# SwiGLU feed-forward block: the first weight loads wait for the issue of x, and the first two gate groups run ahead of the up groups

## The chip, the cores and the metric

The kernel runs on one core of a Trainium2 chip. The metric is the device time of the program in microseconds (us). A core has TensorE (PE in the profile, with its weight loads shown apart as PEld), VectorE (DVE), ScalarE (ACT), GpSimd (POOL) and SyncE (SP). In this kernel SP and ACT issue all the DMAs. Their transfers run on 16 shared DMA engines, from one queue for each issuer: q1 for SP and q10 for ACT.

## The reference

The inputs are bf16: x of [1, 2048, 512], w_gate and w_up of [512, 1376], w_down of [1376, 512].

```python
def reference(x, w_gate, w_up, w_down):
    g = _silu(x @ w_gate)
    u = x @ w_up
    return (g * u) @ w_down
```

## The kernel before, in words

**Layout.** TensorE multiplies along the partitions, so x is needed transposed: `xT_sb` holds it as four slices of 128 features (dk = 0 to 3) by 2048 tokens. The tokens are cut into four chunks of 512. `w_sb` holds w_gate and, behind it, w_up. The 1376 hidden features are ten full tiles of 128 (ft = 0 to 9) and a rest of 96, which is packed into groups of its own ("X" and "Y").

**Groups.** A group is one PSUM bank's worth of work. For a full tile and a chunk there is a gate group ("G") and an up group ("U"), each of four matmuls of 128x128 weights against 512 columns of x. ScalarE takes silu of the gate bank (L280), and VectorE multiplies this with the up bank into `hT_sb` (L289). After all chunks come the groups of the down projection ("O", L394 and L408), whose banks are copied to `o_sb` (L293) and stored by SP (L258). There are 8 banks, used in turn.

**Loads.** The first 256 tokens of x are loaded untransposed into `xn_sb` (L108), and TensorE transposes them by an identity matrix (L346). The second 256 tokens come by a transposing DMA named `x0b` (`load_x`, L87), as do the later chunks. The weights come in slabs of tiles, a gate half and an up half each: `wg0` and `wu0` are tile 0, `wg1` and `wu1` tile 1, then tiles 2 and 3, 4 to 6, and 7 to the end (`load_w`, L92). ScalarE issues `wg0` and `wu0` as the first thing it does (`loads_on_scalar`), and then loads its activation table and runs a dummy activation (L269). SyncE issues everything else in this order (`loads_on_sync`): `xn`, `wg1`, `wu1`, `x0b`, the other slabs, the x of the later chunks, and w_down. An engine issues in the order of its program; a `wait_ge` ahead of an issue holds whatever stands behind it on that engine.

**TensorE's opening** (`on_tensor`). First come N_WARM = 6 matmuls of 512 columns and N_FILL = 2 of 128 on constants (L337), whose results are not used. Then TensorE waits for the identity and for `xn`, and does eight 128x128 transposes (L346): for the token pieces i = 0 and 1 (128 tokens each) and the halves h = 0 and 1 of the features. Each pair goes to a bank, and VectorE (h = 0) or ScalarE (h = 1) copies it to `xT_sb`. The four first groups, g0, u0, g1 and u1 (gate and up of tiles 0 and 1, chunk 0), then run by pieces of columns through `gu_matmuls(g, n0, n1)` (L328): g0 on piece 0 and on piece 1 (4 matmuls of 128 columns each), u0 likewise, then g1 and u1 on both pieces at once (4 matmuls of 256 columns each), and last the second half (tokens 256 to 511, from `x0b`) of g0, u0, g1 and u1, 4 matmuls of 256 columns each. From there the groups run whole. `need(name)` makes TensorE wait for a load when it is first used, and `after` for a copy; both are waits of the first matmul that needs them. No planner decides this order: it is as written.

Of the kernel before, what the change touches and what calls it, by code (L numbers as in the profile page):

```python
# [6 lines left out]
BF16 = mybir.dt.bfloat16  # L7
FP32 = mybir.dt.float32

N_WARM = 6  # L10
N_FILL = 2


def bass_standalone__swiglu_ffn__prompt_kernel(nc, x, w_gate, w_up, w_down, out):
    _, S, D = x.shape
    F = w_gate.shape[1]
    P = 128
# [11 lines left out]
    HT = SC // 2  # L29
    NXN = HT // P  # L30
# [14 lines left out]
    with ExitStack() as es:  # L45
        sb = lambda name, shape, dt: es.enter_context(nc.sbuf_tensor(name, shape, dt))
        ps = lambda name, shape, dt: es.enter_context(nc.psum_tensor(name, shape, dt))
        sem = lambda name: es.enter_context(nc.semaphore(name))
# [18 lines left out]
        diag = sb("diag", [P, P], mybir.dt.int32)  # L67

        s_I = sem("s_I")
        s_J = sem("s_J")  # L70
        s_P = sem("s_P")
        s_A = sem("s_A")
# [4 lines left out]
        def load_sem(name):  # L77
            loads[name] = sem(f"s_{name}")
            return loads[name]
# [6 lines left out]
        def load_x(eng, name, t0, t1):  # L86
            eng.dma_start_transpose(  # L87
                xT_sb[:, :, t0:t1], xf[t0:t1, :]
            ).then_inc(load_sem(name), 16)

        def load_w(eng, name, src, base, f0, f1):
            eng.dma_start(  # L92
                w_sb[:, :, base + f0:base + f1],
                src[:, f0:f1].rearrange("(k p) f -> p k f", p=P),
            ).then_inc(load_sem(name), 16)
# [4 lines left out]
        def load_slab(eng, a, b):  # L100
            load_w(eng, f"wg{a}", w_gate, 0, a * P, min(b * P, F))
            load_w(eng, f"wu{a}", w_up, UPH, a * P, min(b * P, F - 32))

        def loads_on_scalar(act):
            load_slab(act, *slabs[0])

        def loads_on_sync(sp):
            sp.dma_start(  # L108
                xn_sb[:, :, :].rearrange("p j d -> p (j d)"), xf[0:HT, :].rearrange("(p j) d -> p (j d)", j=NXN)
            ).then_inc(load_sem("xn"), 16)  # L110
            load_slab(sp, *slabs[1])
            load_x(sp, "x0b", HT, SC)
            for a, b in slabs[2:]:
                load_slab(sp, a, b)
            load_w(sp, "wut", w_up, F - (F - 32), F - 32, F)
            for c in range(1, NSC):
                load_x(sp, f"x{c}", c * SC, (c + 1) * SC)
            sp.dma_start(
                wd_sb[:, 0:NFF, :], w_down[0:NFF * P, :].rearrange("(k p) d -> p k d", p=P)
            ).then_inc(load_sem("wd"), 16)  # L120
            for c in range(NSC):
                sp.dma_start(
                    wdt_sb[R * c:R * (c + 1), :, :], w_down[NFF * P:F, :].rearrange("(q p) d -> p q d", p=R)
                ).then_inc(load_sem(f"wdt{c}"), 16)
            sp.dma_start(wdl_sb[:, :], w_down[NFF * P:F, LASTA:D]).then_inc(load_sem("wdl"), 16)
# [7 lines left out]
        def add_group(kind, **what):  # L133
            g = dict(kind=kind, at=len(groups), bank=banks[len(groups) % NB], readers=[], **what)
            groups.append(g)
            return g
# [71 lines left out]
        for i in range(NXN):  # L208
            for h, eng in enumerate("DA"):
                g = add_group("T", i=i, h=h)  # L210
                op = add_op(
                    eng, g, kind="copy", out=xT_sb[:, 2 * h:2 * h + 2, i * P:(i + 1) * P],
# [15 lines left out]
        for at in range(NST):  # L228
# [5 lines left out]
            for c0, c1 in halves:  # L234
                g = add_group("O", t=t, c0=c0, c1=c1, c=c)
                if c0 == 0:
                    quads[j].append(g)
                else:
# [3 lines left out]
                    eng, g, kind="copy", out=o_sb[ob][:, c0:c1], src=g["bank"][:, 0:c1 - c0],  # L242
# [11 lines left out]
        def on_sync(sp):  # L254
            loads_on_sync(sp)
            for t, c0, c1, ob, eng, n in stores:
                sp.wait_ge(s_A if eng == "A" else s_D, n)
                sp.dma_start(rows_of(t)[:, c0:c1], o_sb[ob][:, c0:c1]).then_inc(s_out[ob], 16)  # L258
            for i in range(NOS):
                sp.wait_ge(s_out[i], 16 * n_store[i])  # L260
# [6 lines left out]
        def on_scalar(act):  # L267
            loads_on_scalar(act)
            act.activation(adummy[:, 0:4], zero_c, ACT.Silu)  # L269
            for op in act_ops:  # L270
                act.wait_ge(s_P, op["g"]["at"] + 1)
                if op["kind"] == "silu":
                    if op["free"]:
                        act.wait_ge(s_D, op["free"])
                    fn = ACT.Silu
                else:
                    if op["stored"][1]:
                        act.wait_ge(*op["stored"])
                    fn = ACT.Copy
                act.activation(op["out"], op["src"], fn).then_inc(s_A, 1)  # L280
# [15 lines left out]
        def on_tensor(pe):  # L296
            landed = set()

            def need(name):
                if name not in landed:  # L300
                    pe.wait_ge(loads[name], 16)
                    landed.add(name)
# [3 lines left out]
            def after(eng, n):  # L306
                if n > read[eng]:
                    pe.wait_ge(s_A if eng == "A" else s_D, n)
                    read[eng] = n
# [6 lines left out]
            def gu_matmuls(g, n0, n1):  # L316
                c, ft = g["c"], g["ft"]
                if c > 0:
                    need(f"x{c}")
                if c == 0 and n1 > HT:  # L320
                    need("x0b")
                need(("wg" if g["kind"] == "G" else "wu") + str(slab_of[ft]))
                col = (0 if g["kind"] == "G" else UPH) + ft * P
                for dk in range(KD):
                    if c == 0 and dk % 2 == 0:
                        for i in range(n0 // P, min(n1 // P, NXN)):
                            after(*xt_ready[i, dk // 2])
                    ins = pe.matmul(  # L328
                        g["bank"][:, n0:n1], lhsT=w_sb[:, dk, col:col + P],
                        rhs=xT_sb[:, dk, c * SC + n0:c * SC + n1], start=(dk == 0), stop=(dk == KD - 1),  # L330
                    )
                if n1 == SC:
                    ins.then_inc(s_P, 1)

            def warm(n, width):
                for i in range(n):
                    pe.matmul(banks[NB - 1][:, 0:width], lhsT=ones_w, rhs=ones_m[:, 0:width], start=True, stop=True)  # L337

            warm(N_WARM, SC)
            warm(N_FILL, P)  # L340
# [6 lines left out]
                ins.then_inc(s_P, 1)  # L347

            g0, u0, g1, u1 = groups[NT:NT + 4]
            for g in (g0, u0):  # L350
                gu_matmuls(g, 0, P)
                gu_matmuls(g, P, HT)
            gu_matmuls(g1, 0, HT)
            gu_matmuls(u1, 0, HT)
            for g in (g0, u0, g1, u1):
                gu_matmuls(g, HT, SC)
# [80 lines left out]
        on_gpsimd(nc.gpsimd)  # L437
        on_scalar(nc.scalar)
        on_tensor(nc.tensor)
        on_vector(nc.vector)  # L440

# [27 lines left out]
```

## Time and profile before

| what | value |
|---|---|
| median of 3 runs | 120.57 us (120.52 to 120.98) |
| the profiled execution's own time | 120.32 us |
| its span, first to last instruction | 118.9 us (so 1.42 us lie around it) |
| TensorE matmul busy | 115.4 us (97%) |
| TensorE weight loads busy | 54.1 us (45%) |
| VectorE, ScalarE busy | 47.3 us (40%), 31.0 us (26%) |
| SP queue q1, ACT queue q10 | 8.48 MB, 0.26 MB |

How to read the views used below. All times count from the span's start. A row of the timeline is the start, the duration, the engine with the source line, the operation with output<-inputs and shape, the number of instructions merged into the row, and in brackets the idle time before it and what ended that. An engine name with a q (SPq, ACTq) is its issue of a DMA, not the transfer. A row of the stretch view is a stretch A:B with its length, then each engine's busy time and instructions, then the granted clock, the DMA engines' mean busy share, and the GB/s moved. The DMA view gives packets and MB by queue. Matmul ends are modelled, and matmuls overlap, so the starts of weight loads (PEld) are the better clock of TensorE.

### The profile page before, as it was taken

What the parts mean: (1) busy time and instruction counts of PE and PEld (TensorE: products, weight loads), DVE (VectorE), ACT (ScalarE), POOL (GpSimd) and SP (SyncE); (2) the same over time, 40 slices, a digit from 0 to 9 for tenths busy, and PEclk for the clock granted to TensorE, in tenths of its full rate; (3) what the DMA queues carried; (4) which work ended last, traced back from release to release, by engine and by line L of the source; (5) the groups of instructions that cost most, each with busy time, mean ns of one, the idle gap of its engine ahead of it and who ended that gap; (6) DMA issues with size and microseconds to landing.
All of it is one profiled execution on the core that took longest, in us unless ns stands there. A gap on an engine that the chain in (4) does not pass through costs nothing.

```text
span 118.9 us, 1519 instructions
## 1 busy us (share of the span) xinstructions
PE 115.4 (97%) x600; PEld 54.1 (45%) x611; DVE 47.3 (40%) x73; ACT 31.0 (26%) x53; POOL 0.4 (0%) x5
## 2 busy tenths in 40 slices
PE   7999999999999999999999999999999999999993
PEld 2774444444444444444444444344434444444452
DVE  0133443353443444433444334469617422006530
ACT  4344324454234363244262343230000000000001
POOL 1000000000000000000000000000000000000000
PEclk9999999999999999999999999999999999999999
DMA  3999999970000000000000000000004221002412
GB/s 103 271 307 357 264 162 242 328 183 24 0 0 0 6 0 0 0 3 3 0 0 0 6 0 0 0 0 0 0 0 138 88 88 44 0 0 75 145 50 88
DMA packets 17559, 8.84 MB, mean 74 GB/s; under 512 B 10640, under 2 KB 17424, under 8 KB 17552
## 3 DMA queue, kind: packets, MB, share of 16 engines
q1 hardware_dynamic: 16496, 8.48, 26.7%
q10 hardware_dynamic: 1056, 0.26, 1.0%
q8 instruction: 5, 0.08, 0.3%
q14 instruction: 2, 0.02, 0.1%
HBM read 4.81 MB, written 2.10 MB: 58 GB/s over the span
## 4 chain that ended last, share of the span: by engine, by line
PE 97%; issue 1%; DVE 0%
PE bank L328 58%; PE bank L394 29%; PE bank L370 3%; PE bank L337 2%; PE bank L408 2%; PE bank L381 2%; PE bank L346 1%; DVE o_sb L293 0%; PE bank L431 0%
## 5 line engine op out<-in xcount | busy, mean ns | idle before, releaser
L328 PE MATMUL bank<-xT_sb,w_sb 128*128 128x512 bf16 (+2 forms) x338 | 69.7, 364 | 0.4
L328 PEld LDWEIGHTS bank<-xT_sb,w_sb 128*128 128x128 bf16 x344 | 32.8, 98 | 36.4 <-issue 0.2
L289 DVE TENSOR_TENSOR hT_sb<-sg_sb,bank 128x512 bf16<-128x512 f32 x40 | 27.5, 688 | 40.5 <-PE bank L328 36.6
L394 PE MATMUL bank<-wd_sb,hT_sb 128*128 128x512 bf16 (+2 forms) x166 | 34.5, 366 | 0.4 <-issue 0.3
L280 ACT ACTIVATE sg_sb<-bank 128x512 f32<-128x512 f32 x40 | 23.8, 596 | 40.8 <-PE bank L328 40.8
L394 PEld LDWEIGHTS bank<-wd_sb,hT_sb 128*128 128x128 bf16 x170 | 16.1, 98 | 19.1 <-issue 1.3
L293 DVE CAST o_sb<-bank 128x512 bf16<-128x512 f32 (+1 forms) x16 | 10.1, 663 | 22.0 <-PE bank L408 12.3
L280 ACT ACTIVATE o_sb<-bank 128x384 bf16<-128x384 f32 x1 | 0.5, 492 | 37.8 <-PE bank L394 37.8
L289 DVE TENSOR_TENSOR ht_sb<-sgy_sb,bank 32x512 bf16<-32x512 f32 x8 | 5.5, 684 | 0.2
L289 DVE TENSOR_TENSOR ht_sb<-sgx_sb,bank 32x512 bf16<-32x512 f32 x4 | 2.8, 691 | 3.5 <-ACT sgx_sb L280 3.5
L370 PE MATMUL bank<-xT_sb,w_sb 128*128 128x512 bf16 x15 | 4.1, 379 | 0.1
L337 PE MATMUL bank<-const-bfloat16-1.0 128*128 128x512 bf16 (+1 forms) x8 | 2.9, 545 | 0.8 <-PEq L454 0.8
L280 ACT ACTIVATE sgx_sb<-bank 32x512 f32<-32x512 f32 x4 | 2.4, 588 | 4.5 <-PE bank L370 4.5
L408 PE MATMUL bank<-wdt_sb,ht_sb 32*128 32x512 bf16 (+1 forms) x48 | 2.9, 372 | 0.0
L370 PEld LDWEIGHTS bank<-xT_sb,w_sb 128*128 128x128 bf16 x16 | 1.6, 98 | 1.9
L280 ACT ACTIVATE sgy_sb<-bank 64x512 f32<-64x512 f32 x4 | 2.4, 590 | 0.1
L337 PEld LDWEIGHTS bank<-const-bfloat16-1.0 128*128 128x128 bf16 x8 | 1.0, 136 | 2.4 <-issue 2.4
L381 PE MATMUL bank<-xT_sb,w_sb 128*64 128x512 bf16 x16 | 1.9, 382 | 0.0
L408 PEld LDWEIGHTS bank<-wdt_sb,ht_sb 32*128 32x128 bf16 x48 | 1.1, 93 | 1.7 <-issue 0.8
L269 ACT ACT_TABLE_LOAD x1 | 1.3, 1283 | 1.8 <-issue 1.8
L293 DVE COPY xT_sb<-bank 128x256 bf16<-128x256 bf16 x2 | 0.6, 292 | 2.7 <-PE bank L346 2.7
L381 PEld LDWEIGHTS bank<-xT_sb,w_sb 128*64 128x64 bf16 x16 | 0.8, 109 | 1.0 <-DVE hT_sb L289 0.4
(14 smaller groups left out, 4.0 us busy)
## 6 DMA issues: line engine op xcount, KB each, us to landing
out_dram<-o_sb SPq DMA_DIRECT2D x15, 128.0 KB, 1.7
wd_sb<-in_w_down_dram SPq DMA_DIRECT2D x1, 1280.0 KB, 9.2
w_sb<-in_w_gate_dram SPq DMA_DIRECT2D x1, 480.0 KB, 5.9
w_sb<-in_w_up_dram SPq DMA_DIRECT2D x1, 448.0 KB, 6.5
w_sb<-in_w_gate_dram SPq DMA_DIRECT2D x1, 384.0 KB, 4.5
w_sb<-in_w_up_dram SPq DMA_DIRECT2D x1, 384.0 KB, 5.1
wdt_sb<-in_w_down_dram SPq DMA_DIRECT2D x4, 96.0 KB, 7.5
xn_sb<-in_x_dram SPq DMA_DIRECT2D x1, 256.0 KB, 2.8
```

What stands on the lines that cost most here:

```text
L269: act.activation(adummy[:, 0:4], zero_c, ACT.Silu)
L280: act.activation(op["out"], op["src"], fn).then_inc(s_A, 1)
L289: ins = dve.tensor_tensor(op["out"], op["a"], op["b"], ALU.mult)
L293: ins = dve.tensor_copy(op["out"], op["src"])
L328: ins = pe.matmul(g["bank"][:, n0:n1], lhsT=w_sb[:, dk, col:col + P], rhs=xT_sb[:, dk, c * SC + n0:c * SC + n1], start=(dk == 0), stop=(dk ...
L337: pe.matmul(banks[NB - 1][:, 0:width], lhsT=ones_w, rhs=ones_m[:, 0:width], start=True, stop=True)
L346: ins = pe.transpose(tview(g["bank"])[:, k, :], xn_sb[:, g["i"], dk * P:(dk + 1) * P], ident[:, :])
L370: ins = pe.matmul(g["bank"][:, :], lhsT=w_sb[:, dk, XC0:XC0 + P], rhs=xT_sb[:, dk, c * SC:(c + 1) * SC], start=(dk == 0), stop=(dk == KD - 1),
L381: ins = pe.matmul(g["bank"][y0:y1, :], lhsT=w_sb[:, dk, YC0:YC0 + 64], rhs=xT_sb[:, dk, c * SC:(c + 1) * SC], start=(dk == 0), stop=(dk == ...
L394: ins = pe.matmul(g["bank"][:, 0:c1 - c0], lhsT=hT_sb[:, fk, t * P:(t + 1) * P], rhs=wd_sb[:, fk, c0:c1], start=(start and fk == 0), stop= ...
L408: ins = pe.matmul(g["bank"][:, 0:c1 - c0], lhsT=ht_sb[R * c:R * (c + 1), q, j * P:(j + 1) * P], rhs=wdt_sb[R * c:R * (c + 1), q, c0:c1], s ...
```

## The change

One warm-up matmul of 512 columns is removed. ScalarE waits for a new semaphore `s_K` ahead of its first weight load; SyncE counts it up right behind its issue of `xn`, ahead of `wg1`. And the first halves run in another order: g0 and g1 on piece 0, g0 and g1 on piece 1 (16 matmuls of 128 columns), then u0 and u1 on both pieces at once (8 matmuls of 256 columns). The numbers of matmuls of each width stay as they were, apart from the warm-up; the second halves keep their order.

```diff
-N_WARM = 6
+N_WARM = 5
...
+        s_K = sem("s_K")
...
         def loads_on_scalar(act):
+            act.wait_ge(s_K, 1)
             load_slab(act, *slabs[0])
...
             ).then_inc(load_sem("xn"), 16)
+            sp.sem_inc(s_K, 1)
             load_slab(sp, *slabs[1])
             load_x(sp, "x0b", HT, SC)
...
             g0, u0, g1, u1 = groups[NT:NT + 4]
-            for g in (g0, u0):
-                gu_matmuls(g, 0, P)
-                gu_matmuls(g, P, HT)
-            gu_matmuls(g1, 0, HT)
+            for i in range(NXN):
+                for g in (g0, g1):
+                    gu_matmuls(g, i * P, (i + 1) * P)
+            gu_matmuls(u0, 0, HT)
             gu_matmuls(u1, 0, HT)
             for g in (g0, u0, g1, u1):
                 gu_matmuls(g, HT, SC)
```

## The prediction, made before the changed kernel ran

> **What bounds the kernel now.** I read the page first: the chain of work that ended last is 97% PE and the slowest groups are PE's own. So past the opening the kernel is one stream of matmuls, and the change, which touches only the opening, can move the end only by the moment from which that stream runs without a hole. I then read the timeline of the opening:
>
> ```profile
> 0.73 0.46 ACTq L92 DMA_DIRECT2D w_sb<-in_w_gate_dram  x1
> 0.74 0.40 SPq L108 DMA_DIRECT2D xn_sb<-in_x_dram  x1
> ...
> 1.20 0.41 SPq L92 DMA_DIRECT2D w_sb<-in_w_gate_dram  x1
> 1.22 0.53 ACTq L92 DMA_DIRECT2D w_sb<-in_w_up_dram  x1
> ...
> 1.66 0.50 SPq L92 DMA_DIRECT2D w_sb<-in_w_up_dram  x1
> 1.78 1.28 ACT L269 ACT_TABLE_LOAD   x1 [1.78 <-issue]
> ...
> 2.20 1.69 SPq L87 DMA_TRANSPOSE xT_sb<-in_x_dram  x1
> ...
> 3.29 0.15 PEld L337 LDWEIGHTS bank<-const-bfloat16-1.0 128*128 128x128 bf16 x1 [0.28 <-issue]
> 3.60 0.63 PEld L346 LDWEIGHTS bank<-ident,xn_sb 128*128 128x128 bf16 x8 [0.16 <-issue]
> ...
> 4.22 0.66 ACT L280 ACTIVATE xT_sb<-bank 128x256 bf16<-128x256 bf16 x2 [0.94 <-PE bank L346]
> 4.44 1.81 PEld L328 LDWEIGHTS bank<-xT_sb,w_sb 128*128 128x128 bf16 x24 [0.21 <-issue]
> ...
> 6.42 7.47 PEld L328 LDWEIGHTS bank<-xT_sb,w_sb 128*128 128x128 bf16 x44 [0.17 <-DMA xT_sb<-in_x_dram]
> ```
>
> The reader is to see three starts: transposes at 3.60, the first gate matmul behind the load at 4.44, and the second halves at 6.42. The bracket of the last row is the point of the case: PE stood waiting for x0b. The DMA view says that x0b landed 4.2 us after its issue, 2.20 + 4.2 = 6.4. So PE had nothing to do until x0b came, if only just: the last of the 24 loads ends at 4.44 + 1.81 = 6.25, its matmul of 256 columns then runs for 0.11 (the pace is worked out below), to about 6.37, so the hole is 0.05 us. **Whatever is gained ahead of 6.37 is given back at x0b.** Later loads are early: wg2 lands near 7.2 (issue 3.94 and 3.3), and is due behind 16 matmuls of 256 columns, near 8.2.
>
> What sets x0b? Its queue is SP's: xn, wg1, wu1, x0b, 768 KB, beside 256 KB of ACT's. The stretches show how the 1 MB moves, and the queues of two windows, 0 to 2.5 us and 2.5 to 3 us, who moved it:
>
> ```profile
> 1.50:2.00 0.50, 0.50 (x2) 0.15 (x1) 0.00 (x0) 0.22 (x1) 0.00 (x0) 1.00 0.29 102
> 2.00:2.50 0.50, 0.50 (x3) 0.21 (x2) 0.00 (x0) 0.50 (x1) 0.00 (x0) 1.00 1.05 320
> 2.50:3.00 0.50, 0.50 (x3) 0.22 (x2) 0.00 (x0) 0.50 (x1) 0.00 (x0) 1.00 0.86 199
> 3.00:3.50 0.50, 0.50 (x4) 0.16 (x2) 0.00 (x0) 0.27 (x2) 0.00 (x0) 1.00 1.07 229
> 3.50:4.00 0.50, 0.50 (x6) 0.40 (x5) 0.00 (x0) 0.00 (x0) 0.00 (x0) 1.00 1.26 285
> 4.00:4.50 0.50, 0.43 (x7) 0.29 (x6) 0.46 (x2) 0.28 (x2) 0.00 (x0) 1.00 1.28 286
> ```
> ```profile
> q1 hardware_dynamic: 103, 0.21, 26.8%
> q10 hardware_dynamic: 1, 0.00, 0.0%
> ```
> ```profile
> q10 hardware_dynamic: 196, 0.05, 44.9%
> q1 hardware_dynamic: 35, 0.05, 41.1%
> ```
>
> From 3.5 us the engines move a level 286 GB/s. By 2.5 us, 103 of the 128 packets of xn (2 KB each) are through and ACT's queue has only just begun; from 2.5 to 3 xn's last 25 share the engines with 196 small packets of wg0, at 199 GB/s.
>
> **The change part by part.**
>
> *The wait.* SP's issue of xn ends at 0.74 + 0.40 = 1.14. SP's steps from one issue to the next are 0.06, so I take 0.06 for the count and 0.06 for ACT's waking: ACT issues wg0 at 1.26 instead of 0.73, 0.53 later. Bounds: 1.14 (nothing for either) and about 1.4. SP's own issues, wg1 to all later ones, move by 0.06, x0b to 2.26. Behind ACT's wait stand wg0, wu0, the table load and the dummy activation: the table's end moves from 3.06 to 3.59, the dummy's (0.20) to 3.81. ACT's first copy was at 4.22 and could come at about 3.85 now, so this still hides, by 0.04; without that cover ACT's copies would be late by what is missing.
>
> *xn.* Alone, its last 25 packets (50 KB at 320 GB/s, 0.16 us) are through at 2.66 rather than beyond 3.0. xn landed at 0.74 + 2.8 = 3.54. I take 3.15; the bounds are 3.1 and 3.54 (no gain).
>
> *The warm-up matmul.* Loads of the 512-wide warm-up are 0.43 apart (2.86, 3.29), so one less ends PE's filler at about 3.07 instead of 3.50. With xn at 3.15 the transposes start at about 3.2, 0.4 earlier, and end near 4.1 (eight at a quarter of 0.43); with the copies' 0.2 behind them gate 0 could start near 4.3. Bounds: a gain of 0.43, or nothing where xn stays at 3.54.
>
> *wg0.* It landed 3.2 after its issue: now 1.26 + 3.2 = 4.46, and with 0.09 from landing to the first matmul, as for xn (3.54 to 3.63), gate 0 starts at 4.55, where it was 4.47. So the 0.4 of the transposes is not cashed: **the wait moves the stop from x to wg0.** Bounds: 4.3 (wg0 comes no later than the copies), and 5.0 if wg0 and wg1, now issued in the same instant, split the engines (128 KB more at 286 GB/s is 0.46).
>
> *The order.* Same matmuls, so it costs nothing itself; it moves due dates. At the later full pace (229 matmuls in the 49.79 busy us of 20 to 70, 0.217 for 512 columns, so 0.054 for 128 and 0.109 for 256) the first halves take 16 x 0.054 + 8 x 0.109 = 1.74 us; before they took 6.37 - 4.47 = 1.90 with small waits for copies. wg1 is now due behind 4 matmuls, 4.77, and lands at 1.26 + 3.4 = 4.66: 0.1 of cover, where it had 0.9. wu0 is due at 4.55 + 0.87 = 5.42 and lands at 1.75 + 3.7 = 5.45: a hole of 0.03 at most by these rows. wu1 is due at 5.87 and lands at 5.42. So PE reaches the second halves at 6.29 (4.55 + 1.74) to 6.45 (+ 1.90).
>
> *x0b.* The megabyte ahead of its landing is the same, and so is the start at 1.8. ACT's first packet came at 2.50, 1.77 after its issue; the same interval now gives 3.03. wg1's packets came about 3.0 (SP's other 10 packets of that window are the most there can be before), and now come near 3.1. So between 2.66 and 3.03 the engines would stand idle, and at 3.0 they are 196 x 256 B = 50 KB behind, 0.18 us at 286 GB/s. In 3.0 to 3.5 two queues now start together and can make up at most (286 - 229) x 0.5 = 28 KB, 0.10 us. That leaves +0.08 to +0.18; I take **+0.12**. Bounds: if the 1.77 was only a place in a line, so that wg1 moves up, the engines could run level from 2.5, and (286 - 199) x 0.5 + (286 - 229) x 0.5 = 72 KB come 0.25 us earlier; at the other end the whole 0.53 and SP's 0.06 stay idle, +0.59. The value lies nearest to the packets' own rows.
>
> [...]
>
> **The sum.** PE resumes at the later of x0b (6.42 + 0.12 = 6.54) and its own arrival (6.29 to 6.45): 6.54, 0.12 later. Behind it nothing differs. The profiled execution took 120.32 (118.9 of span, 1.42 around it), so 120.44; the median of the runs lies 0.25 above it, and by the median it is 120.57 + 0.12, about **120.7 us**.
>
> **The rivals.**
> 1. *The engines fill sooner* (wg1 takes the place of wg0): x0b up to 0.25 earlier, and wg0 by 4.4. For it: xn is alone, and two queues start together. Against it: of SP's 35 packets from 2.5 to 3, 25 are xn's, so at most 10 of wg1's 512 moved before 3.0, though it was issued at 1.20. 120.3 to 120.57. Chance 0.22.
> 2. *The weights collide*: wg0 and wg1 split the engines, gate 0 starts at 5.0, arrival 6.8, or x0b takes the whole delay. For it: wg1's cover has shrunk to 0.1. Against it: wu0's later due date. +0.3 to +0.59, 120.9 to 121.2. Chance 0.13.
> 3. *The clock comes later* (the slower side). TensorE starts at half pace: 0.43 for 512 columns against 0.217 later, although the clock column reads 1.00. It doubles inside the transposes: five of their loads take 3.60 to 4.05, the last two are 0.06 apart. So 3.2 us after the first matmul at 0.77 the clock was granted. If the shorter filler no longer earns it, it comes 3.2 us later, at 7.2; from 4.55 to 7.2, 2.65 us at half pace lose 1.3 us: 120.57 + 1.3 = 121.9. It decides at about 4.0 us. [...] Against it: the busy time to 4.0 stays about the same. Chance 0.10. [...]
> 4. *It doesn't do what it says*: xn lands at 3.54 all the same. Then PE idles 0.47 ahead of the transposes, and gate 0 starts near 4.55 as by wg0. The time is the forecast's, and is counted with it.
>
> **How the numbers follow.** Forecast, +0 to +0.3: 0.55. The range runs from rival 1 less 0.1 for the runs' own spread, 120.2, to the top of rival 2, 121.2; it leaves out rival 3 and small tails. A measurement of this kernel can tell about 0.5% (0.6 us) from no change. Faster by that needs more than any bound here: 0.03. Slower: rival 3 and a tail of rival 2, 0.12. Within: 0.85.
>
> **What would show it.** Right: ACT's first issue near 1.26, transposes near 3.2, first gate matmul near 4.55 behind wg0, and PE's load at the second halves near 6.54, ended by x0b. Wrong: gate 0 near 4.3; a hole before the 5th or 17th matmul (wg1, wu0) over 0.1; 512-wide pace not reached by 4.5; or second halves that start without x0b in the bracket.

## The result, and the profile after

The changed kernel takes 121.12 us (median of 20 runs, 120.69 to 122.6), the kernel before 120.61 us (20 runs, 120.28 to 121.31). The ratio is **1.0037, 95% interval 1.0021 to 1.0053**: slower by 0.45 us, 0.25 to 0.64. The forecast was 0.12 us slower. (Runs in a slower state that executions here can fall into, one at 122.6 us here and three of 12 near 123.2 in the experiment of the wait alone, stand in the medians but not in the ratios.)

The profiled execution took 121.02 us with a span of 119.6, 0.7 more than before. (That of before, 120.32 us, lies 0.29 below its median, so the two profiles differ by more than the medians do.) The timeline of its opening, the rows that answer to those shown of before:

```profile
0.74 0.40 SPq L110 DMA_DIRECT2D xn_sb<-in_x_dram  x1
...
1.22 0.50 ACTq L93 DMA_DIRECT2D w_sb<-in_w_gate_dram  x1
1.25 0.39 SPq L93 DMA_DIRECT2D w_sb<-in_w_gate_dram  x1
...
1.74 0.55 ACTq L93 DMA_DIRECT2D w_sb<-in_w_up_dram  x1
...
2.25 1.70 SPq L88 DMA_TRANSPOSE xT_sb<-in_x_dram  x1
...
3.82 0.77 PEld L349 LDWEIGHTS bank<-ident,xn_sb 128*128 128x128 bf16 x8 [0.81 <-issue]
...
4.67 1.37 PEld L331 LDWEIGHTS bank<-xT_sb,w_sb 128*128 128x128 bf16 x16
...
6.25 7.70 PEld L331 LDWEIGHTS bank<-xT_sb,w_sb 128*128 128x128 bf16 x49 [0.21 <-DMA w_sb<-in_w_up_dram]
```

Three things are to be seen. The filler ends earlier, but the transposes start at 3.82 where they started at 3.60: x did not come sooner, and TensorE idles 0.81 us for it. The 16 loads of the gate pieces start at 4.67. And the stop that ends last is no longer x0b: the bracket at 6.25 names the up half of tile 0, **wu0**. From there the first halves of u0 and u1 still have to run, 8 x 0.109 = 0.87 us, so the second halves start at 7.12, 0.70 later than the 6.42 of before: the whole 0.7 us of the span. Only the sixteen gate matmuls could run ahead of it. x0b was late too: it landed at 2.25 + 4.8 = 7.05, so it would by itself have held the second halves to about the same moment.

The DMA view of the issues up to 3 us, with the KB and the time from issue to landing, has the reason:

```profile
xn_sb<-in_x_dram SPq DMA_DIRECT2D x1, 256.0 KB, 3.0
w_sb<-in_w_gate_dram ACTq DMA_DIRECT2D x1, 128.0 KB, 3.3
...
w_sb<-in_w_up_dram SPq DMA_DIRECT2D x1, 128.0 KB, 4.0
w_sb<-in_w_up_dram ACTq DMA_DIRECT2D x1, 128.0 KB, 4.5
xT_sb<-in_x_dram SPq DMA_TRANSPOSE x1, 4.8
```

wu0 was issued 0.52 later than before (1.74 against 1.22) and then took 4.5 instead of 3.7 us; x0b took 4.8 instead of 4.2. The stretches of after show when the engines slowed (the last two columns are their busy share and GB/s):

```profile
1.50:2.00 0.50, 0.50 (x2) 0.15 (x1) 0.00 (x0) 0.00 (x0) 0.00 (x0) 1.00 1.03 57
2.00:2.50 0.50, 0.50 (x3) 0.21 (x2) 0.00 (x0) 0.18 (x1) 0.00 (x0) 1.00 0.39 86
2.50:3.00 0.50, 0.50 (x4) 0.22 (x2) 0.00 (x0) 0.50 (x1) 0.00 (x0) 1.00 0.92 333
3.00:3.50 0.50, 0.28 (x3) 0.01 (x1) 0.00 (x0) 0.50 (x1) 0.00 (x0) 1.00 1.22 301
...
4.00:4.50 0.50, 0.50 (x7) 0.50 (x6) 0.24 (x1) 0.03 (x1) 0.00 (x0) 1.00 1.05 222
4.50:5.00 0.50, 0.50 (x8) 0.33 (x6) 0.34 (x2) 0.46 (x2) 0.00 (x0) 1.00 1.11 243
5.00:5.50 0.50, 0.50 (x7) 0.50 (x7) 0.00 (x0) 0.28 (x1) 0.00 (x0) 1.00 1.41 248
5.50:6.00 0.50, 0.50 (x11) 0.50 (x8) 0.00 (x0) 0.00 (x0) 0.00 (x0) 1.00 1.25 204
```

and those of before behind 4.5 us:

```profile
4.50:5.00 0.50, 0.50 (x8) 0.37 (x9) 0.12 (x1) 0.38 (x2) 0.00 (x0) 1.00 1.28 287
5.00:5.50 0.50, 0.50 (x11) 0.50 (x11) 0.00 (x0) 0.00 (x0) 0.00 (x0) 1.00 1.29 279
5.50:6.00 0.50, 0.50 (x8) 0.45 (x6) 0.00 (x0) 0.00 (x0) 0.00 (x0) 1.00 1.11 250
```

From 2.5 to 3.5 us, where I feared idle engines, they moved more than before (333 and 301 GB/s against 199 and 229), but from 1.5 to 2.5 less (57 and 86 against 102 and 320). The two nearly cancel: over these 2 us the mean is 194 GB/s against 212, and the kernels without the wait lie on both sides of it (188 to 217 in seven profiles). The larger loss comes from 4.0 on: 222, 243, 248 and 204 against 286, 287, 279 and 250. In the window 4.5 to 6 us before, ACT's queue had 2 packets left; here it has 469, so wu0 (ACT's queue) now overlaps the transposing x0b (SP's queue).

### The profile page after: what moved, and what is told of

Read it like the earlier page. It is cut to its first block, busy times and chain, and to the rows that moved or that the text cites. A ratio compares the mean times of both kernels' runs of the same rounds, so it can differ in the third digit from the quotient of the medians.

```text
span 119.6 us, 1529 instructions
## 1 busy us (share of the span) xinstructions
PE 116.3 (97%) x610; PEld 54.5 (46%) x610; DVE 47.2 (40%) x73; ACT 31.1 (26%) x53; POOL 0.4 (0%) x5
## 4 chain that ended last, share of the span: by engine, by line
PE 95%; DMA 2%; DVE 0%; issue 0%
PE bank L331 58%; PE bank L397 29%; PE bank L373 3%; DMA xn_sb<-in_x_dram 2%; PE bank L411 2%; PE bank L384 2%; PE bank L349 1%; DVE o_sb L296 0%; PE bank L434 0%
## 5 line engine op out<-in xcount | busy, mean ns | idle before, releaser
L331 PEld LDWEIGHTS bank<-xT_sb,w_sb 128*128 128x128 bf16 x344 | 33.3, 99 | 36.3 <-DMA w_sb<-in_w_up_dram 0.2
L397 PE MATMUL bank<-wd_sb,hT_sb 128*128 128x512 bf16 (+2 forms) x170 | 35.1, 367 | 0.0
L296 DVE CAST o_sb<-bank 128x512 bf16<-128x512 f32 (+1 forms) x16 | 10.1, 663 | 22.0 <-PE bank L411 12.3
L373 PEld LDWEIGHTS bank<-xT_sb,w_sb 128*128 128x128 bf16 x16 | 1.6, 98 | 1.9
L349 PE MATMUL bank<-ident,xn_sb 128*128 128x128 bf16 x8 | 1.0, 305 | 0.6 <-DMA xn_sb<-in_x_dram 0.6
```

Source lines behind the costliest of these rows:

```text
L296: ins = dve.tensor_copy(op["out"], op["src"])
L331: ins = pe.matmul(g["bank"][:, n0:n1], lhsT=w_sb[:, dk, col:col + P], rhs=xT_sb[:, dk, c * SC + n0:c * SC + n1], start=(dk == 0), stop=(dk ...
L349: ins = pe.transpose(tview(g["bank"])[:, k, :], xn_sb[:, g["i"], dk * P:(dk + 1) * P], ident[:, :])
L373: ins = pe.matmul(g["bank"][:, :], lhsT=w_sb[:, dk, XC0:XC0 + P], rhs=xT_sb[:, dk, c * SC:(c + 1) * SC], start=(dk == 0), stop=(dk == KD - 1),
L397: ins = pe.matmul(g["bank"][:, 0:c1 - c0], lhsT=hT_sb[:, fk, t * P:(t + 1) * P], rhs=wd_sb[:, fk, c0:c1], start=(start and fk == 0), stop= ...
```

## The experiments

Two theories stood against each other. **Theory A**: the wait makes the loss, by the lateness of wu0 and x0b. **Theory B**: the shorter filler makes the loss, because TensorE's full pace (0.217 us for 512 columns instead of 0.43) is granted later. All comparisons are with runs of before on the same chip; a ratio of 1.001 is 0.12 us. What the expectations call a look is one profiled execution.

### The wait alone, and the order alone

The wait and the count alone, in the kernel before:

```diff
         def loads_on_scalar(act):
+            act.wait_ge(s_K, 1)
             load_slab(act, *slabs[0])
...
+            sp.sem_inc(s_K, 1)
             load_slab(sp, *slabs[1])
```

> Before plus the wait alone (six warm-up matmuls, old order). Theory A (the wait moves wg0 and wu0 behind SP's loads, and PE stands for wu0 and x0b): slower than before by 0.3 to 0.6 us; more in the old order than in the new, since u0 is due 0.45 us earlier here: PE stands about 1 us ahead of u0. Theory B (one warm-up matmul less lets PE idle ahead of the transposes, and the full pace comes late): within 0.15 us of before, full pace reached by about 4.2 us.

Measured: 121.33 us, ratio **1.0054 (1.0034 to 1.0075)**, +0.65 us. Theory A is borne out in kind: the timeline has TensorE standing for wu0, at u0's first half, right behind the first eight gate matmuls. It stands 0.53 us, half of what was expected, and the loss is a little above the expected range.

```profile
4.66 0.78 PEld L331 LDWEIGHTS bank<-xT_sb,w_sb 128*128 128x128 bf16 x8
5.97 2.09 PEld L331 LDWEIGHTS bank<-xT_sb,w_sb 128*128 128x128 bf16 x24 [0.53 <-DMA w_sb<-in_w_up_dram]
```

The order alone, in the kernel before:

```diff
-            for g in (g0, u0):
-                gu_matmuls(g, 0, P)
-                gu_matmuls(g, P, HT)
-            gu_matmuls(g1, 0, HT)
+            for i in range(NXN):
+                for g in (g0, g1):
+                    gu_matmuls(g, i * P, (i + 1) * P)
+            gu_matmuls(u0, 0, HT)
```

> Before with the new order of the first halves alone. Both theories: within 0.15 us of before; wg1 (landing near 4.6) is due at about 4.7, so a stop of up to 0.1 us ahead of the fifth matmul may show, hidden by x0b near 6.4.

Measured: 120.54 us, ratio 1.0003 (0.9984 to 1.0022). As expected, the order costs nothing by itself.

### Each of the other two parts taken back

After without the wait and the count:

```diff
-            act.wait_ge(s_K, 1)
...
-            sp.sem_inc(s_K, 1)
```

> After without the wait and the count (five warm-up matmuls and the new order stay). Theory A: back to before within 0.15 us, whatever PE idles ahead of the transposes, since wg0 lands near 3.9 and x0b near 6.4 as before. Theory B: slower than before by 0.3 to 0.5 us, the pace of weight loads doubles only near 5.7 us.

Measured: 120.84 us, ratio 1.0010 (0.9984 to 1.0036), single runs from 120.19 to 121.48. wu0 and x0b landed as before, near 4.9 and 6.4. In its profile the pace of weight loads doubled only near 6.7 us, and that execution took 121.15. The median favours theory A, the profile shows the late full pace of theory B, and the interval excludes neither.

After with the sixth warm-up matmul back:

```diff
-N_WARM = 5
+N_WARM = 6
```

> After with the sixth warm-up matmul back (wait and new order stay). Theory A: as slow as after, 0.3 to 0.6 us above before, with PE standing ahead of u0 for wu0. Theory B: back to before within 0.15 us, full pace near 4.0 us.

Measured: 120.85 us, ratio **1.0020 (1.0002 to 1.0037)**, +0.24 us: half of after's loss is left, between the two theories. The profiled execution was the fastest of the 12 (120.39 us, span 119.1), and it shows hardly any loss: the first gate load waits for wg0, and the second halves for x0b, at 6.46, which is the course that the prediction drew. wu0 took 3.7 us and x0b 4.2, as before, with the same loads issued at the same moments as in after.

```profile
4.49 1.79 PEld L331 LDWEIGHTS bank<-xT_sb,w_sb 128*128 128x128 bf16 x24 [0.29 <-DMA w_sb<-in_w_gate_dram]
6.46 1.53 PEld L331 LDWEIGHTS bank<-xT_sb,w_sb 128*128 128x128 bf16 x15 [0.18 <-DMA xT_sb<-in_x_dram]
```

Yet the two transfers overlapped here too. By 4.5 us SP's queue had moved 1177 packets. The 128 of xn and the 512 each of wg1 and wu1 make 1152, so nearly all that followed is x0b. The stretch from 4.5 to 5 us, and its queues:

```profile
4.50:5.00 0.50, 0.48 (x9) 0.49 (x10) 0.10 (x1) 0.36 (x2) 0.00 (x0) 1.00 1.28 286
q1 hardware_dynamic: 290, 0.07, 64.7%
q10 hardware_dynamic: 288, 0.07, 63.1%
```

x0b and the last packets of wu0 ran side by side at 286 GB/s.

By the medians: set beside the wait in the old order (+0.65), the new order gives back 0.41 us. Where wu0 sets the end, that is what it should: behind u0's start the old order has 8 x 0.054 + 8 x 0.109 = 1.31 us of first halves left, the new one 0.87, and the difference is 0.44.

### The filler by itself

```diff
-N_WARM = 6
+N_WARM = 5
```

> Before with five warm-up matmuls alone. Theory A (the wait is all of the loss): within 0.1 us of before. Theory B (the shorter filler makes the full pace come later on average): slower by 0.1 to 0.3 us, with single runs up to 121.5, since the pace doubled only near 6.7 us in the look at the kernel without the wait.

Measured: 120.72 us, ratio 1.0017 (0.9998 to 1.0036), +0.20 us, -0.02 to +0.43: inside theory B's range, and not quite clear of nothing. So I took the dose:

```diff
-N_WARM = 6
+N_WARM = 2
```

> Before with two warm-up matmuls instead of six, nothing else: the dose of theory B. The filler ends near 1.8 us and TensorE idles till xn lands near 3.5. Theory B: the full pace is granted only about 3.2 us after the transposes start, near 6.8, and from 4.5 to 6.8 half the work is lost: slower by 0.7 to 1.3 us. Theory A: within 0.15 us of before, since xn, wg0 and x0b land as before.

Measured: 122.0 us, ratio **1.0109 (1.0071 to 1.0147)**, +1.3 us. The filler matters. The stretches of its profile, 6.5 to 8.7 and 8.9 to 10.1 us, show the step: 11 weight loads in 2.20 us, then 12 in 1.20, on matmuls of one width (256 columns), although the clock column says 1.00 in both.

```profile
6.50:8.70 2.20, 2.20 (x12) 1.53 (x11) 0.00 (x0) 0.00 (x0) 0.00 (x0) 1.00 1.03 275
8.90:10.10 1.20, 1.20 (x14) 1.07 (x12) 0.32 (x1) 0.75 (x2) 0.00 (x0) 1.00 1.06 353
```

### A second profile of each kernel

The kernel before, unchanged:

> Before, unchanged, for a second look at it. If the moment of the full pace is fixed by the program, it doubles near 4.0 us again, as in the first look. If it is luck between executions, it comes anywhere up to some 3 us later, and the execution is longer by half of what it comes after 4.5.

Measured: 120.64 us with a span of 119.2. The pace doubled near 5.5 us, not 4.0: the moment moves between executions of one kernel, and this execution took 0.3 us more. After, unchanged:

> After, unchanged, for a second look. Theory B: the pace of weight loads doubles later than in any look with six warm-up matmuls (3.9 to 5.5 us), as it did in the three with five (5.7, 6.4, 6.7). Theory A: xn near 3.6, no earlier than without the wait; wu0 between 5.4 and 6.2, after its due date, and x0b at 6.4 to 7.0.

Measured: 120.99 us, span 119.6. Here theory B's expectation **failed**: the pace doubled near 4.1 us, about as early as in the first profile of before, and the execution was as long as the first. Its timeline:

```profile
4.46 1.01 PEld L331 LDWEIGHTS bank<-xT_sb,w_sb 128*128 128x128 bf16 x16 [0.20 <-DMA w_sb<-in_w_gate_dram]
6.23 1.86 PEld L331 LDWEIGHTS bank<-xT_sb,w_sb 128*128 128x128 bf16 x18 [0.77 <-DMA w_sb<-in_w_up_dram]
```

The 16 gate loads now take 1.01 instead of 1.37 us, and TensorE then stands 0.77 instead of 0.21 us for wu0, until 6.23 instead of 6.25. In both profiles of after wu0 is the last stop, and an earlier full pace is given back at that wait. (xn landed 2.8 after its issue, at 3.5; wu0 4.4 after, x0b 4.7. x0b came at 2.25 + 4.7 = 6.95, only some 0.1 ahead of the moment to which wu0 held the second halves.)

### What makes wu0 and x0b late

The wait between ScalarE's two loads, so that wg0 goes out early and wu0 late:

```diff
-            load_slab(act, *slabs[0])
+            a, b = slabs[0]
+            load_w(act, f"wg{a}", w_gate, 0, a * P, min(b * P, F))
+            act.wait_ge(s_K, 1)
+            load_w(act, f"wu{a}", w_up, UPH, a * P, min(b * P, F - 32))
...
-            load_slab(sp, *slabs[1])
+            a, b = slabs[1]
+            load_w(sp, f"wg{a}", w_gate, 0, a * P, min(b * P, F))
+            sp.sem_inc(s_K, 1)
+            load_w(sp, f"wu{a}", w_up, UPH, a * P, min(b * P, F - 32))
```

> Before (six warm-up matmuls, old order) with the wait between ScalarE's two loads: wg0 goes out at 0.73 as before, wu0 waits for a count that SyncE makes behind the issue of wg1, so that it goes out near 1.7, where the whole wait put it. If the lateness of wu0 makes the loss of the wait (theory A in its narrow form): gate 0 starts near 4.45, PE stands 0.4 to 0.8 us ahead of u0, and the time is 0.4 to 0.7 us above before, as with the whole wait in the old order. If it is wg0's lateness or the engines' idle time at the front: within 0.2 us of before.

Measured: 120.77 us, ratio 1.0020 (1.0001 to 1.0038), +0.24 us. Less than the narrow form of theory A asked for, more than its opposite: wu0 landed at 5.5, 3.8 after its issue, and TensorE stood 0.24 us for it; x0b landed at 6.7. So a late issue of wu0 alone makes about a third of the loss of the whole wait. There wu0 took 4.2 us and came at 5.9; what slowed it this run does not tell. But it has a slow stretch of its own:

```profile
5.00:5.50 0.50, 0.44 (x6) 0.13 (x3) 0.00 (x0) 0.10 (x1) 0.00 (x0) 1.00 1.38 181
q1 hardware_dynamic: 355, 0.09, 137.6%
```

181 GB/s, with SP's queue alone: ACT's last packet had gone by 5.0. So in this profile the engines slowed beside x0b with nothing in the other queue.

wu0 moved to SyncE's queue, between wg1 and wu1, in the kernel of the wait alone:

```diff
         def loads_on_scalar(act):
             act.wait_ge(s_K, 1)
-            load_slab(act, *slabs[0])
+            a, b = slabs[0]
+            load_w(act, f"wg{a}", w_gate, 0, a * P, min(b * P, F))
...
             sp.sem_inc(s_K, 1)
-            load_slab(sp, *slabs[1])
+            a, b = slabs[1]
+            load_w(sp, f"wg{a}", w_gate, 0, a * P, min(b * P, F))
+            a, b = slabs[0]
+            load_w(sp, f"wu{a}", w_up, UPH, a * P, min(b * P, F - 32))
+            a, b = slabs[1]
+            load_w(sp, f"wu{a}", w_up, UPH, a * P, min(b * P, F - 32))
```

> The kernel of e1 (wait, six warm-up matmuls, old order), but wu0 issued by SyncE between wg1 and wu1, and so in one queue with x0b; ScalarE issues wg0 alone, behind the wait. If in the looks with the wait wu0's packets were held up beside the transposing transfer of x0b in the other queue: wu0 lands near 5.0 to 5.4, PE stands under 0.4 us ahead of u0, and the time is 0.1 to 0.4 us above before instead of e1's 0.65. If it is the late issue of wg0 and the engines' start that cost: 0.5 us or more above before, since x0b is also issued 0.5 us later.

Measured: 121.0 us, ratio 1.0031 (1.0013 to 1.0048), +0.37 us, in the range that the side-by-side reading asked for. TensorE never stood for wu0, and the engines moved 271 GB/s from 4 to 6 us, like the kernels without the wait. x0b took 3.9 us instead of 4.6 to 4.8, but it was also issued 0.54 later, at 2.79, and so landed at 6.7, near the 6.85 of the wait alone. Everything behind x0b on SyncE had moved back as well, and the loss reappears there, at tile 2's gate weights (issued at 4.58 instead of 3.94, and 4.3 instead of 3.3 us from issue to landing):

```profile
8.93 0.55 PEld L337 LDWEIGHTS bank<-xT_sb,w_sb 128*128 128x128 bf16 x4 [0.53 <-DMA w_sb<-in_w_gate_dram]
9.68 0.23 PEld L337 LDWEIGHTS bank<-xT_sb,w_sb 128*128 128x128 bf16 x2 [0.20 <-DMA w_sb<-in_w_up_dram]
```

So this run moves the loss to another place and does not decide between the two readings.

### x with the engines to itself

```diff
+            sp.wait_ge(loads["xn"], 16)
             sp.sem_inc(s_K, 1)
```

> The kernel of e1 (wait, six warm-up matmuls, old order), with SyncE also waiting until xn has landed before it counts and issues anything else, so that xn has the DMA engines to itself. If sharing with wg0 made xn late (the step of the prediction), xn lands near 3.1. If xn's time is its own, it lands near 3.5 to 3.7, as in all looks with and without the wait. The weights and x0b come some 2.5 us late, so the time is 2 to 3 us above before and says nothing.

Measured, one execution (124.29 us): **xn landed 2.8 us after its issue, at 3.5**, as without the wait. The DMA view of 0 to 3 us has SP's queue only, and xn still took as long:

```profile
q1 hardware_dynamic: 136, 0.25, 25.6%
issues: line engine op xcount, KB each, median us to landing
xn_sb<-in_x_dram SPq DMA_DIRECT2D x1, 256.0 KB, 2.8
```

So in this execution there was nothing for the wait to win. Its profile also shows the clock itself, in its column (third from the right) of three stretches:

```profile
3.65:7.05 3.40, 1.01 (x16) 0.84 (x16) 0.51 (x2) 2.04 (x4) 0.00 (x0) 1.00 0.74 157
7.07:10.46 3.39, 2.81 (x20) 2.10 (x18) 0.00 (x0) 0.00 (x0) 0.00 (x0) 0.50 1.19 274
10.48:14.00 3.52, 3.47 (x26) 2.38 (x25) 1.38 (x2) 1.79 (x3) 0.00 (x0) 1.00 1.09 371
```

It was granted near 3.6 (the loads of its eight transposes, from 3.64, take 0.46 us where the first profile of before needed 0.63), taken away after 3.4 us in which TensorE had been busy for 1.01, and granted again 3.4 us later. The dates of the full pace in two profiles of one kernel lie 1.5 us apart for before (4.0 and 5.5) and 1.6 for after (5.7 and 4.1). What sets the date within one kernel was not shown.

### An attempt to do better

```diff
-N_FILL = 2
+N_FILL = 4
...
                 ins.then_inc(s_P, 1)
+            warm(2, P)
```

> Before with two more 128-wide filler matmuls behind the warm-up and two behind the transposes, in stretches where TensorE stood idle (3.50 to 3.60 and 4.24 to 4.44 in the first look). Theory B: the full pace comes earlier on average, and the time is 0.05 to 0.3 us below before. If the filler only delays the transposes and gate 0, at half pace by up to 0.2 us each: 0.1 to 0.3 us above before. Theory A says nothing on it.

Measured: 120.66 us, ratio 1.0009 (0.9991 to 1.0027): no difference that these runs can tell. The pace doubled near 5.5 us in its profile. No version here is shown to beat the kernel before.

## Why the prediction was right, and where it was wrong

**Right: the direction, the size class, and the frame.** Only the opening moved the end, and by the last stop ahead of the unbroken stream. Of the terms: ACT's first issue came at 1.22 (1.26 forecast), and the first gate load at 4.67 and 4.46 in the two profiles (4.55 forecast). In the second it waits for wg0, as forecast; in the first it follows the transposes, which x held up. The order costs nothing alone (1.0003) and takes 0.41 us off the price of the wait.

**In part luck.** The time lies in the range, but at its top: 121.12 us is in the band of rival 2 (120.9 to 121.2, chance 0.13), not in the forecast's own (+0 to +0.3). And it got there neither by the forecast's path nor by rival 2's first branch (gate 0 at 5.0), but by wu0, with an x0b that took the whole delay. Three of the prediction's signs of being wrong came true: a hole of more than 0.1 ahead of the 17th matmul (0.21 and 0.77 us), in the first profile a full pace only at 5.7, and second halves whose last named stop is wu0 instead of x0b.

**Wrong: the size, 0.12 against 0.45 us.** The step that failed is the due date of wu0: "lands at 1.75 + 3.7 = 5.45: a hole of 0.03 at most". I carried over the 3.7 us that wu0 took before. In after it took 4.5 and 4.4 us, landed at 6.2, and set the end: PE's own arrival at the second halves became 7.12 and 7.10 instead of 6.29 to 6.45. The second term of that sum was off by nearly as much: x0b at 7.05 and 6.95, about 0.6 later where +0.12 was taken.

What slowed these two transfers is open. From 4 to 6 us the engines moved 270 to 285 GB/s in the seven profiles without the wait, and 210 to 253 in four of the five in which the wait put wu0 late on ACT's queue (after twice, the wait alone, and wu0 alone held back). So the slow stretch goes with the late wu0. But running beside x0b is not enough to explain it: after with six warm-up matmuls ran both side by side at 286 GB/s and moved 283 over the 2 us (wu0 3.7, x0b 4.2), and with wu0 alone held back the slowest half microsecond, 181 GB/s, came when ACT's queue was empty. The same loads at the same moments thus gave a span 0.7 us longer in two profiles and 0.2 in a third. The wait's price is a mean over such draws, and the prediction took one draw for a fixed duration.

**Wrong: x earlier.** "Alone, its last 25 packets are through at 2.66", landing 3.15. It landed at 3.5 to 3.7 in every profile, with the wait or without, and at 3.5 when quite alone. From 2.0 to 2.5 us, with hardly a packet but xn's moving, the engines gave 86 GB/s in after and 82 in after without the wait; the 320 of before came in only one of the other profiles (319, with more filler), and between 82 and 193 in the rest. What holds xn in that stretch isn't settled.

**Right in kind, wrong in place: x0b.** It came about 0.6 later, at the top of my bounds. But I had put the loss at the front, to engines idle for want of ACT's packets, where rival 1's mechanism (wg1 takes the free place: it landed 3.0 after its issue instead of 3.4) did fill them. By 3.5 us the wait shows no loss beyond the spread of the kernels without it (194 and 205 GB/s from 1.5 to 3.5 us in after, 188 to 217 without). The loss came behind 4 us. With ACT's loads held back, x0b came about when it had come before (6.40) in the profile with six warm-up matmuls (2.24 + 4.2 = 6.44), and at 7.05 and 6.95 in the two of after: the bytes are the same and the rate is not (283 GB/s from 4 to 6 us, against 229 and 210).

**Rival 3, the clock, is real, and was priced too much as one step.** Four matmuls fewer cost 1.3 us. One fewer costs about 0.20 us, which the interval doesn't separate from nothing. The full pace came at 3.6 to 5.5 us in the profiles with six or more warm-up matmuls, at 4.1, 5.7, 6.4 and 6.7 with five, at 8.8 with two. My reason "decides at about 4.0" took one draw for a fixed date; beyond the length of the filler, no run shows what the grant goes by.

**The sum as measured.** The wait in the new order +0.24 (the kernel with six warm-up matmuls) and the shorter filler +0.20 (alone) make 0.44, against 0.45 for the change. In single executions the two overlap: in the two profiles of after TensorE stood for wu0 until 6.25 and 6.23, so a full pace at 5.7 instead of 4.1 cost nothing. So the split holds for the means only, and the 0.20 is not settled.

## What to carry to other kernels

Ahead of holding one transfer back for another, find out what the other takes alone: here x took as long when it was quite alone (2.8 us, against 2.8 to 3.0 beside other loads), and the wait only made the weights late. A duration from issue to landing that is read from one profile is one draw, for the company and the moment of that execution (wu0 took 3.7, 4.2, 4.4 and 4.5 us in the four profiles with the whole wait and wu0 on ACT's queue): where a load falls due within a tenth of a microsecond of its landing, a forecast needs the spread of several profiles. The same holds for the moment at which TensorE's pace doubles (4.0 and 5.5 us in two profiles of before): profile the same kernel twice ahead of reading a date from it.

## What the runs showed of the hardware that I had not expected

- With a 128 KB load held back by half a microsecond, the 16 DMA engines moved 210 to 253 GB/s from 4 to 6 us in four profiles of five, at a busy share up to 1.41, where 270 to 285 were moved without the wait. Two queues side by side are not the reason by themselves: one profile had both at 286 GB/s, and another fell to 181 with one queue alone.
- In the profile of x alone the full clock was granted near 3.6 us, taken back 3.4 later and granted again after 3.4 more. The clock column reads 1.00 ahead of the first grant too, when a matmul of 512 columns takes 0.43 us instead of 0.217: the starts of the weight loads tell it.
- A load of 256 KB into idle engines took 2.8 us from issue to landing, no less than beside others (2.8 to 3.0).
